# Splitting the last matmul of a decode layer 6 to 8 instead of 4 to 10 over the TensorE column groups, and issuing two of its blocks earlier

## The chip, the cores and the metric

One core of a Trainium2 chip. The metric is device microseconds (us) of one execution; a time is the median of several executions. The profile's span runs from the first to the last instruction and is about 1.8 us shorter than the measured time.

## The reference

A decode step of one transformer layer, for four rows (batch 4, one token): modulated layer norm, attention over the last 1024 cached keys and values, then a feed-forward part with ReLU. Only its end matters here:

```python
h = layernorm(x) * (1 + cb) + sb
x = x + gb * (relu(h @ w1) @ w2)     # w1: 512 x 1792, w2: 1792 x 512, bf16
```

The kernel reads 32 MB of weights and caches for very little arithmetic.

## The kernel before

All large loads go through one queue, in the order of use. w2 comes last, in five transfers. It has 14 **blocks** of 128 rows, numbered m = 0 to 13.

```python
nc.sync.dma_start(out=w1_sb, in_=B_w1.rearrange("(p t) n -> p t n", t=DT))
W2_CHUNKS = [(0, 4), (4, 4), (8, 3), (11, 2), (13, 1)]      # (first block, blocks)
for (m0, e) in W2_CHUNKS:
    nc.sync.dma_start(out=w2_dst[:, m0 * D:(m0 + e) * D],
                      in_=B_w2[m0 * P:(m0 + e) * P, :].rearrange("(q e) n -> q (e n)", e=e))
```

The product with w2 has four useful rows, so the kernel uses TensorE in column groups of 32. A block takes two steps (x = 0, 1), and in each step one matmul in each of two groups. The lower pair of groups (0, 1) accumulates into `z_ps`, the upper pair (2, 3) into `za_ps`.

```python
def closing(parts):
    for x in range(NX):                                   # NX = 2
        for (ps, q, j, src, rhs, start, stop, cols) in parts:
            for g in range(2):
                q0 = (q + g) * CG                         # column group q + g, CG = 32
                nc.tensor.matmul(out=ps[q0:q0 + CG, cols], lhsT=rows(src, j, x), rhs=rhs(2 * x + g),
                                 start=start and x == 0, stop=stop and x == NX - 1, tile_position=(0, q0))
...
for (m0, m1) in [(0, 8), (8, FT)]:                        # FT = 14
    ffn1(m0, m1)                                          # uT32 = relu(h @ w1), in two parts
for m in range(ZA):                                       # ZA = 4
    closing([zpart(m), zpart(ZA + m)])                    # upper m beside lower 4 + m
zc = work.tile([2 * CG, DH2], f32, name="zc")             # the side path
nc.scalar.copy(out=zc[:], in_=za_ps[2 * CG:P, :])
nc.vector.tensor_tensor(out=zc[:], in0=zc[:], in1=gb2[:], op=ALU.mult)
nc.vector.tensor_tensor(out=zc[:], in0=zc[:], in1=x12_ps[:], op=ALU.add)
for m in range(2 * ZA, FT):
    closing([zpart(m)])                                   # blocks 8 to 13, lower
zg = work.tile([2 * CG, DH2], f32, name="zg")
nc.vector.tensor_tensor(out=zg[:], in0=z_ps[:], in1=gb2[:], op=ALU.mult)
nc.vector.tensor_tensor(out=res[:], in0=zg[:], in1=zc[:], op=ALU.add)
# then res is stored from two queues
```

Of the kernel before, what the change touches and what calls it, by code (L numbers as in the profile page):

```python
# [17 lines left out]
def kernel(  # L18
# [23 lines left out]
    FT = Dff // P  # L42
# [13 lines left out]
    DH2 = D // NH  # L56
# [65 lines left out]
    w2_sb = w12[:, DT * Dff:DT * Dff + FT * D].rearrange("p (m n) -> p m n", m=FT)  # L122
# [54 lines left out]
    uT32 = const.tile([P, FT, CP], bf16, name="uT32")  # L177
# [8 lines left out]
    def rows(tile3, j, x):  # L186
        return tile3[:, j, NX - x:NX - x + CG]

    def closing(parts):
        for x in range(NX):  # L190
            for (ps, q, j, src, rhs, start, stop, cols) in parts:
                for g in range(2):
                    q0 = (q + g) * CG
                    nc.tensor.matmul(out=ps[q0:q0 + CG, cols], lhsT=rows(src, j, x), rhs=rhs(2 * x + g),  # L194
                                     start=start and x == 0, stop=stop and x == NX - 1, tile_position=(0, q0))
# [272 lines left out]
        return w1_sb[:, t, m0 * P + m - m0:(m0 + e) * P:e]  # L468


    ZA = 4
    z_ps = psA.tile([2 * CG, DH2], f32, tag="t", name="z_ps")
    za_ps = psA.tile([P, DH2], f32, tag="t", name="za_ps")

    def ffn1(m0, m1):
        u_ps = psA.tile([P, m1 - m0, 2, B], f32, tag="t", name=f"u_ps_{m0}")
        for m in range(m0, m1):
            for t in range(DT):
                nc.tensor.matmul(out=u_ps[:, m - m0].rearrange("p s b -> p (s b)"), lhsT=w1_cols(t, m),
                                 rhs=ab[:, t].rearrange("p s b -> p (s b)"), start=(t == 0), stop=(t == DT - 1))  # L480
        us = work.tile([P, m1 - m0, B], f32, name=f"us_{m0}")
        nc.vector.tensor_tensor(out=us[:], in0=u_ps[:, :, 0, :], in1=rstd2[:].unsqueeze(1).to_broadcast([P, m1 - m0, B]),
                                op=ALU.mult)
        nc.vector.tensor_tensor(out=us[:], in0=us[:], in1=u_ps[:, :, 1, :], op=ALU.add)
        nc.vector.tensor_scalar_max(out=put(uT32[:, m0:m1, :]), in0=us[:], scalar1=0.0)

    def zpart(m):
        upper = m < ZA
        return (za_ps if upper else z_ps, 2 if upper else 0, m, uT32, lambda j: w2_sb[:, m, j * DH2:(j + 1) * DH2],
                m in (0, ZA), m in (ZA - 1, FT - 1), slice(None))  # L490

    for (m0, m1) in [(0, 8), (8, FT)]:
        ffn1(m0, m1)
    for m in range(ZA):
        closing([zpart(m), zpart(ZA + m)])
    zc = work.tile([2 * CG, DH2], f32, name="zc")
    nc.scalar.copy(out=zc[:], in_=za_ps[2 * CG:P, :])
    nc.vector.tensor_tensor(out=zc[:], in0=zc[:], in1=gb2[:], op=ALU.mult)
    nc.vector.tensor_tensor(out=zc[:], in0=zc[:], in1=x12_ps[:], op=ALU.add)
    for m in range(2 * ZA, FT):  # L500
        closing([zpart(m)])

    zg = work.tile([2 * CG, DH2], f32, name="zg")
# [36 lines left out]
```

## Time and profile before

| | before |
|---|---|
| time, median of 3 runs | 85.59 us (85.52 to 85.87) |
| span of the profiled execution | 83.9 us |
| landings of the w2 transfers 1 to 5, from the trace | 77.16, 78.45, 79.36, 80.03, 80.35 us |
| first and last z matmul start | 78.49, 80.58 us |
| zg, res, store issued | 80.93, 81.25, 81.56 us |

A landing can be read off the page's views: the start of the issue in the queue's timeline plus the time from issue to landing.

### The profile page before, as it was taken

Reading aid. Unit: us, or ns where it says so; the run is one execution under the profiler, and the core shown is the slowest. Engines: PE = TensorE matmul, PEld = TensorE weight load, DVE = VectorE, ACT = ScalarE, POOL = GpSimd, SP = SyncE. Lnnn points to the kernel's source line nnn. Section 1 sums busy time; section 2 is a strip of 40 time slices with the busy share of each in tenths; the row PEclk is TensorE's granted clock in tenths of the full one; section 3 lists DMA queues with packets and bytes.
Section 4 is the critical chain, followed back from the end, with each engine's and each line's share of the span. In section 5 each row is a group of like instructions: output and inputs, shape, how many; then the busy total and the mean of one; then the engine's idle time right before and its main releaser. Section 6 shows DMA issues by size and latency. Waiting matters only on the chain.

```text
span 83.9 us, 2373 instructions
## 1 busy us (share of the span) xinstructions
PE 56.3 (67%) x1064; PEld 47.6 (57%) x1064; DVE 26.3 (31%) x76; ACT 23.9 (28%) x38; POOL 5.9 (7%) x21
## 2 busy tenths in 40 slices
PE   0001006999972989999999932999737579577850
PEld 0001006995862973997777702999737249567640
DVE  0201300348033010264566576850001320251350
ACT  3201001654302000497779809530100010001000
POOL 5894000000000000000000000000000000000000
PEclk9999999999995555599999999569655555555555
DMA  2799999998999999999999999999999999999600
GB/s 40 287 474 431 390 430 442 512 500 360 391 387 410 430 422 426 403 426 422 418 414 422 422 418 426 410 426 418 422 410 430 410 430 437 408 384 402 233 4 2
DMA packets 4258, 32.14 MB, mean 383 GB/s; under 512 B 529, under 2 KB 665, under 8 KB 1305
## 3 DMA queue, kind: packets, MB, share of 16 engines
q1 hardware_dynamic: 4192, 31.99, 92.1%
q8 instruction: 8, 0.13, 0.6%
q10 hardware_dynamic: 24, 0.01, 0.0%
q0 software_dynamic: 32, 0.00, 0.0%
q14 instruction: 2, 0.01, 0.0%
HBM read 31.99 MB, written 0.00 MB: 382 GB/s over the span
## 4 chain that ended last, share of the span: by engine, by line
DMA 61%; PE 30%; DVE 3%; issue 1%; SPq 1%; ACT 1%; DVEq 0%
DMA v<-in_A_v_cache_dram 24%; DMA w<-in_B_w_dram 23%; PE ktp L225 14%; DMA k<-in_A_k_cache_dram 14%; PE qT_ps L322 4%; PE sc_ps L237 3%; PE z_ps L194 3%; PE mT L273 2%; PE mT L275 1%; PE m_ps L259 1%; PE m_ps L262 1%; PE st_ps_var L289 1%; PE gb_ps L194 1%; SPq L93 0%; SPq L92 0%
## 5 line engine op out<-in xcount | busy, mean ns | idle before, releaser
L225 PE MATMUL ktp<-ident_k,k 128*128 128x128 bf16 x256 | 18.8, 245 | 5.6 <-DMA k<-in_A_k_cache_dram 5.6
L225 PEld LDWEIGHTS <-k 128*128 128x128 bf16 x256 | 17.8, 112 | 8.2 <-DMA k<-in_A_k_cache_dram 5.7
L230 ACT COPY kT<-ktp 128x1024 bf16<-128x1024 bf16 x16 | 15.6, 1015 | 17.9 <-PE ktp L225 16.8
L228 DVE COPY kT<-ktp 128x1024 bf16<-128x1024 bf16 x16 | 11.1, 692 | 16.8 <-PE ktp L225 16.5
L360 PE MATMUL oT_ps<-pT,v 128*128 128x16 bf16 x256 | 7.1, 172 | 2.0 <-issue 2.0
L360 PEld LDWEIGHTS <-v 128*128 128x128 bf16 x256 | 7.1, 100 | 2.0 <-issue 2.0
L237 PE MATMUL sc_ps<-kT,qpad 128*32 128x512 bf16 x64 | 5.6, 445 | 0.4 <-DVE qpad L326 0.4
L377 PE MATMUL pT_ps<-ident_bf,p_rep 128*128 128x128 bf16 x32 | 3.3, 287 | 2.9 <-DVE p_rep L371 2.9
L200 PE MATMUL tp<-ident_bf,cx_sb 8*128 8x8 bf16 x4 | 0.3, 176 | 7.3 <-POOL xs L180 7.3
L377 PEld LDWEIGHTS <-p_rep 128*128 128x128 bf16 x32 | 2.9, 131 | 3.4 <-DVE p_rep L371 3.4
L322 PE MATMUL qT_ps<-hT,wq_sb 128*128 128x4 bf16 x128 | 3.6, 167 | 1.4 <-DVE ab L315 1.4
L200 PEld LDWEIGHTS <-cx_sb 8*128 8x128 bf16 x4 | 0.2, 116 | 7.3 <-DMA cx_sb<-in_A_x_dram 7.3
L322 PEld LDWEIGHTS <-wq_sb 128*128 128x128 bf16 x128 | 3.5, 104 | 1.5 <-DMA wq_sb<-in_A_wq_dram 1.5
L429 ACT COPY y<-y_ps 128x256 f32<-128x256 f32 x1 | 0.4, 372 | 9.3 <-DVE y L428 9.3
L402 DVE TENSOR_TENSOR oT_sb<-oT_ps,rb 128x128 bf16<-128x128 f32 x1 | 0.3, 291 | 7.8 <-PE oT_ps L360 7.8
L436 PEld LDWEIGHTS <-wo_sb 128*128 128x128 bf16 x64 | 2.5, 120 | 0.4 <-DMA wo_sb<-in_A_wo_dram 0.4
L371 DVE TENSOR_TENSOR p_rep<-e_sb,mi 128x512 int32<-128x512 int32 x4 | 2.5, 687 | 0.7 <-ACT e_sb L366 0.7
L436 PE MATMUL y_ps<-o,wo_sb 128*128 128x4 bf16 x64 | 2.4, 173 | 0.4 <-DMA wo_sb<-in_A_wo_dram 0.4
L432 PEld LDWEIGHTS y_ps<-sel_b,y 128*128 128x128 f32 x8 | 1.8, 328 | 1.4 <-DVE y L428 1.4
L194 PEld LDWEIGHTS <-uT 128*32 128x32 bf16 x56 | 2.2, 136 | 0.8 <-DMA w<-in_B_w_dram 0.4
L194 PE MATMUL z_ps<-w,uT 128*32 128x128 bf16 x40 | 2.4, 307 | 0.2 <-DMA w<-in_B_w_dram 0.2
L424 PE MATMUL y_ps<-wo_sb,o 128*32 128x512 bf16 x16 | 1.9, 628 | 0.9 <-DVE o L415 0.9
(113 smaller groups left out, 54.6 us busy)
## 6 DMA issues: line engine op xcount, KB each, us to landing
k<-in_A_k_cache_dram SPq DMA_DIRECT2D x8, 1024.0 KB, 28.4
v<-in_A_v_cache_dram SPq DMA_DIRECT2D x8, 1024.0 KB, 19.8
wq_sb<-in_A_wq_dram SPq DMA_DIRECT2D x1, 4096.0 KB, 23.6
wo_sb<-in_A_wo_dram SPq DMA_DIRECT2D x4, 1024.0 KB, 20.0
wmod_sb<-in_w_mod_dram SPq DMA_DIRECT2D x1, 2304.0 KB, 9.5
w<-in_B_w_dram SPq DMA_DIRECT2D x1, 1792.0 KB
w<-in_B_w_dram SPq DMA_DIRECT2D x2, 512.0 KB, 20.1
wmod_sb<-in_w_mod_dram SPq DMA_DIRECT2D x1, 768.0 KB, 4.4
```

What stands on the lines that cost most here:

```text
L194: nc.tensor.matmul(out=ps[q0:q0 + CG, cols], lhsT=rows(src, j, x), rhs=rhs(2 * x + g), start=start and x == 0, stop=stop and x == NX - 1, ...
L225: nc.tensor.transpose(out=tp[:, ii, :], in_=k_tiles[gi][:, iq * IQ + ii, :], identity=ident_k)
L228: nc.vector.tensor_copy(out=dst, in_=tp[:])
L230: nc.scalar.copy(out=dst, in_=tp[:])
L237: nc.tensor.matmul(out=sc_ps[hw * CG:(hw + 1) * CG, half * HALF:(half + 1) * HALF], lhsT=qpad[:, b, par, hw, :], rhs=kT[:, half * (NI // 2 ...
L322: nc.tensor.matmul(out=qT_v[:, hq, :], lhsT=wq_sb[:, t, hq * Dh:(hq + 1) * Dh], rhs=hT[:, t, :], start=(t == 0 and hq == 0), stop=(t == DT ...
L360: nc.tensor.matmul(out=oT_ps[:, hw, par].rearrange("p b r -> p (b r)"), lhsT=v_tiles[h][:, i, :], rhs=pT[:, i, c0:c0 + B * rep], start=(fi ...
L371: nc.vector.tensor_tensor(out=p_w[:, ws, :], in0=e_w[:, ws].unsqueeze(2).to_broadcast([P, WQ // 2, B]), in1=mi4[:].unsqueeze(1).to_broadca ...
L377: nc.tensor.transpose(out=tp[:, ii, :], in_=p_rep[:, i // 2, :, i % 2], identity=ident_bf[:])
L424: nc.tensor.matmul(out=y4_ps[q0:q0 + CG, :], lhsT=o4[:, l, g % 2, g // 2, :], rhs=wo_sb[:, g, l, :], start=(g == 0 and l < 4), stop=(g == ...
L432: nc.tensor.matmul(out=y_ps[:, t, :], lhsT=y4[:, t, :], rhs=sel_b[:], start=(t == 0), stop=False)
L436: nc.tensor.matmul(out=y_ps[:, m, :], lhsT=wo_sb[:, g, l, m::DT], rhs=o4[:, l, g % 2, g // 2, 0:B], start=False, stop=(g == NP - 1 and l = ...
```

## The change

Its intent is to even out the two pairs of groups, so that fewer matmuls stand in series in the lower pair, and to use the idle time before the second w2 transfer lands for two blocks of the first.

```diff
-    ZA = 4
+    ZUP = (0, 1, 2, 3, 6, 7)
+    ZLOW = tuple(m for m in range(FT) if m not in ZUP)
...
-    for m in range(ZA):
-        closing([zpart(m), zpart(ZA + m)])
+    for ms in [(0,), (1,), (2, 4), (3, 5), (6,), (7,)]:
+        closing([zpart(m) for m in ms])
...
-    for m in range(2 * ZA, FT):
+    for m in range(8, FT):
         closing([zpart(m)])
```

The rest of the diff lets `zpart` pick the pair of groups and the start and stop flags by these lists.

## The prediction

> **What bounds the kernel now.** I read the page's chain that ended last first, then its 40 slices, then the end of the kernel in the chain in order of time and the timeline, and last the table of DMA issues, to set each landing beside the instruction that needs it. The page first:
>
> ```profile
> PEclk9999999999995555599999999569655555555555
> DMA  2799999998999999999999999999999999999600
> ...
> DMA 61%; PE 30%; DVE 3%; issue 1%; SPq 1%; ACT 1%; DVEq 0%
> ```
>
> The reader is to see that the 16 DMA engines are nine tenths busy from the start up to the 37th slice (a slice is 83.9/40 = 2.1 us, so until about 78 us), that DMA is 61% of the chain, and that TensorE runs at a granted clock of 0.5 in all of the last part. This is a kernel that streams weights and caches and ends with what the last bytes leave to do. The last bytes are w2, in five transfers: blocks 0-3, 4-7, 8-10, 11-12 and 13. The change only touches the matmuls on w2, so the end is what I have to read. The chain in order of time:
>
> ```profile
> 58.98 19.47 DMA w<-in_B_w_dram
> 78.45 0.04 issue
> 78.49 0.29 PE z_ps L194 x2
> ...
> 79.44 1.47 PE z_ps L194 x26
> 80.91 0.02 issue
> 80.93 0.29 DVE zg L504
> 81.22 0.02 issue
> 81.25 0.28 DVE res L506
> ```
>
> The second w2 transfer (issued at 58.98) lands at 78.45 and lets the z matmuls go; after them come two DVE steps and the store. Between 78.49 and 80.91 the chain names only PE. That makes TensorE look like the limit there, and the change would then pay. The timeline shows how it works (start, duration):
>
> ```profile
> 77.96 0.29 PE L194 MATMUL za_ps<-w,uT 128*32 128x128 bf16 x2 [0.17 <-DVE uT L485]
> 78.49 0.29 PE L194 MATMUL z_ps<-w,uT 128*32 128x128 bf16 x2 [0.24 <-DMA w<-in_B_w_dram]
> 78.50 0.30 PE L194 MATMUL za_ps<-w,uT 128*32 128x128 bf16 x2
> 78.58 0.32 PE L194 MATMUL z_ps<-w,uT 128*32 128x128 bf16 x2
> 78.58 0.32 PE L194 MATMUL za_ps<-w,uT 128*32 128x128 bf16 x2
> ...
> 79.12 0.32 PE L194 MATMUL za_ps<-w,uT 128*32 128x128 bf16 x2
> 79.48 0.26 ACT L497 COPY zc<-za_ps 64x128 f32<-64x128 f32 x1 [3.56 <-PE za_ps L194]
> ```
>
> A **round** is one matmul in each column group that is in use: 0.107 us from one start to the next ((79.12 - 78.58)/5), whether two groups work or four. Every block needs two rounds in its pair of groups (x = 0 and 1). Before, the lower pair (z_ps) has ten blocks, 20 rounds, and the upper (za_ps) four. Eight z rounds, blocks 4-7, start from 78.49 to 79.22. Then comes block 8, which lies in the third transfer. The issue table and the queue's timeline, narrowed to that issue, and the timeline around 79.4:
>
> ```profile
> w<-in_B_w_dram SPq DMA_DIRECT2D x1, 384.0 KB, 17.9
> ```
>
> ```profile
> 61.49 0.33 SPq L129 DMA_DIRECT2D w<-in_B_w_dram  x1
> ```
>
> ```profile
> 79.22 0.48 PE L194 MATMUL z_ps<-w,uT 128*32 128x128 bf16 x4
> 79.41 0.13 PEld L194 LDWEIGHTS <-uT 128*32 128x32 bf16 x3
> ```
>
> The third transfer lands at 61.49 + 17.9 = 79.39 (rounded), and the next weight loads start at 79.41, though the round that began at 79.22 has streamed its columns by 79.22 + 0.107 = 79.33. Matmul ends are modelled and overlap, so neither chain nor waits show this **0.08 us wait for block 8**; the landing does. In the same way the fourth transfer (256 KB, issued at 64.11, 15.9 us to landing) lands at 80.01, just where block 11 is due: 79.41 + 6 rounds x 0.107 = 80.05. So TensorE is on the chain there, but it is paced by arrivals: block 8 can't start before 79.4, nor block 11 before 80.0.
>
> **What the Trainium skill says.** "TensorE: Matmul & The Clock Gate", Part 3 "The mechanism": "MATMULs are pc-monotone in start AND end"; only weight loads are pulled ahead. So a matmul that waits for a landing holds up those behind it, of other column groups too. The trace agrees: block 0's x = 1 matmuls, whose data were there by 77.96, start at 78.50, behind block 4's wait. "TensorEngine Tiling (Array Packing)", Key Properties: different tiles can run weight loads and matmuls in parallel. The trace agrees: two z and two za matmuls start within 0.01 us and the round is no longer for it. "DMA: Bandwidth & Descriptors", "Why a DMA increments its semaphore by 16 and not by 1": only the full 16 means that all data landed. The kernel waits once for each transfer, so a block can't start on part of one; the trace has single waits at 78.45 and 79.4, but does not show the counts.
>
> **The change part by part.** By the instruction order of both kernels, PE has the same 2020 rows, the same 56 matmuls on w2 and the same waits; DVE and ACT have the same rows in the same order. Nothing is added or removed. Two things move.
>
> 1. Blocks 0 and 1 go first, alone, with the x = 0 matmul pair of block 2 also ahead of the wait for the second transfer: five rounds in the upper groups, from 77.96, about 0.08 for the first and 0.107 for the others (0.08 from the first step above, 78.50 to 78.58): the fifth starts at 77.96 + 0.08 + 3 x 0.107 = 78.36. Before, one round was issued in that gap. So four rounds (0.43 us of TensorE's time) leave the stretch after 78.49 and use idle time. This works, I expect.
>
> 2. Blocks 6 and 7 move from lower to upper: lower has 8 blocks (16 rounds), upper 6 (12). But they are issued as (6,), (7,), with no lower partner. From 78.49: z4 x0 with za2 x1; z4 x1 with za3 x0; z5 x0 with za3 x1; z5 x1 with za6 x0; then za6 x1, za7 x0, za7 x1 alone. That is 7 rounds before block 8 where there were 8, since the za stream is one round ahead. The seventh starts at 78.49 + 0.08 + 5 x 0.107 = 79.11 and block 8's lower groups have been free since about 79.0. So block 8 could start at 79.11 instead of 79.32: in the lower groups 0.107 us for the saved round and another 0.107 because block 8 may run beside za7.
>
> What these are worth: **nothing on the path**, as block 8 still can't start before 79.39. The wait grows from 0.08 to about 0.3 us and the rest stays: block 8 at 79.41, blocks 8-13 in 12 rounds, the last z matmul ending at 80.9, then zg, res and the store. The transfers are issued from 56 to 67 us, long before, and in the same order, so no landing moves. The za path does not move either: the last za round starts at 79.11, as now (79.12), so the copy starts at 79.48, and the two DVE steps on zc end about 80.4, half a microsecond before zg needs DVE. Sum: 0.00 us, give or take 0.03.
>
> **The rivals.** (a) *TensorE is the bound of the end* and the landing at 79.39 is near enough to give way in some runs. Then the most to be had is the wait after the last z round: were all landed, before would go on at 79.32, the changed kernel at 79.11, so 0.1 us for each of the two terms, 0.2 us or 0.25% at most; 85.4 us. For it: the chain names only PE there. Against it: the landing is later than both of these, and DMA has been the limit for the 78 us before, so it comes no earlier because of this change. (b) *The shift of two blocks to za makes the side path late*: the copy of za_ps then comes later and ends after z_ps. It would need over 0.5 us; I count none. If TensorE gave no overlap to za-only rounds, it would be about 0.1 us, still hidden. (c) *A denser burst of matmuls makes the granted clock drop or delays the DVE steps on uT*, which read PSUM while TensorE now writes za_ps. The clock is already 0.5 from before these matmuls to the end; the second uT write is needed only by block 8 (it ends at 78.46), with 0.9 us to spare. Worth 0 to 0.05 us. (d) A scatter of landings between executions of both kernels, which has nothing to do with the change: the runs of before go from 85.52 to 85.87.
>
> **Range and chances.** The centre is before's median, 85.59, less a small share (a fifth) of rival (a): 85.57. The range is mostly the spread of the runs, which is 0.35 us for one kernel; the gain of (a) lies inside it. 85.3 to 85.9. A change of 2% is 1.7 us; the whole stretch from the second landing to the last z matmul is 2.4 us, and the change can't touch over 0.2 of it. So within 2% is nearly certain.
>
> **What would show it right or wrong.** In the changed profile: five za rounds from about 77.96 to 78.4 ahead of the wait for the second transfer; two z blocks in that stretch instead of four; after them za alone to about 79.1; then a gap on TensorE, longer than before, until the third transfer lands at about 79.4; the same 12 rounds to about 80.9; the copy of za_ps at about 79.5 and off the chain. I am wrong if block 8 starts well before the third landing of the profile before (the landing moved), if the za copy ends after zg could start, or if za-only rounds take over 0.107 us, so that block 8 is late by more than 0.05 us.

## The result, and the profile after

| | before | changed |
|---|---|---|
| median of 6 runs | 85.61 us (85.52 to 86.04) | 85.62 us (85.53 to 85.67) |
| second w2 landing | 78.45 | 78.26 |
| third landing, and start of block 8 | 79.36, 79.41 | 79.19, 79.23 |
| last z matmul ends | 80.89 | 80.69 |
| from the second landing to that end | 2.44 | 2.43 |

The ratio of the changed kernel to before is 0.9989, with a 95% interval of 0.9967 to 1.0012: the same. The profiled execution of the changed kernel is 0.2 us ahead of that of before at the second landing already, ahead of anything that changed; so I compare times from that landing on.

The page of the changed kernel, the granted clock and DMA by slices and the chain by engines:

```profile
PEclk9999999999985555799999998589555555555555
DMA  2899999998999999999999999999999999999600
...
DMA 63%; PE 27%; DVE 4%; issue 1%; SPq 1%; ACT 1%; DVEq 0%
```

DMA is busy to the same slice, and TensorE's clock is 0.5 in the last part again. The timeline of the changed kernel (start, duration, engine, line, operation, count):

```profile
77.79 0.72 PE L194 MATMUL za_ps<-w,uT 128*32 128x128 bf16 x10 [0.15 <-DVE uT L486]
...
78.30 0.29 PE L194 MATMUL z_ps<-w,uT 128*32 128x128 bf16 x2
...
78.60 0.32 PE L194 MATMUL z_ps<-w,uT 128*32 128x128 bf16 x2
78.62 0.64 PE L194 MATMUL za_ps<-w,uT 128*32 128x128 bf16 x8
...
79.23 0.45 PEld L194 LDWEIGHTS <-uT 128*32 128x32 bf16 x9 [0.25 <-issue]
79.29 0.26 ACT L498 COPY zc<-za_ps 64x128 f32<-64x128 f32 x1 [3.58 <-PE za_ps L194]
```

The ten za matmuls (five rounds) fill the gap ahead of the second landing. Four z rounds follow, from 78.30 to 78.60, where before had eight; then there are only za rounds. Now there is an idle mark on the weight loads: 0.25 us ahead of 79.23. The view puts it down to "issue", which means only that it found no releaser. The third transfer's issue, in the table of issues and in the queue's timeline, says what it is:

```profile
w<-in_B_w_dram SPq DMA_DIRECT2D x1, 384.0 KB, 17.7
```

```profile
61.46 0.33 SPq L129 DMA_DIRECT2D w<-in_B_w_dram  x1
```

61.46 + 17.7 = 79.16 (79.19 in the trace), and block 8 starts 0.04 us after that, as it did before. The end of the chain is the old one:

```profile
80.71 0.02 issue
80.73 0.29 DVE zg L505
81.03 0.02 issue
81.05 0.28 DVE res L507
```

### The profile page after: what moved, and what is told of

Read it like the earlier page. It is cut to its first block, busy times and chain, and to the rows that moved or that the text cites. A ratio compares the mean times of both kernels' runs of the same rounds, so it can differ in the third digit from the quotient of the medians.

```text
span 83.7 us, 2373 instructions
## 1 busy us (share of the span) xinstructions
PE 56.1 (67%) x1064; PEld 47.0 (56%) x1064; DVE 26.5 (32%) x76; ACT 23.8 (28%) x38; POOL 6.0 (7%) x21
## 4 chain that ended last, share of the span: by engine, by line
DMA 63%; PE 27%; DVE 4%; issue 1%; SPq 1%; ACT 1%; DVEq 0%
DMA w<-in_B_w_dram 26%; DMA v<-in_A_v_cache_dram 24%; DMA k<-in_A_k_cache_dram 14%; PE ktp L225 9%; PE qT_ps L322 4%; PE sc_ps L237 2%; PE z_ps L194 2%; PE mT L273 2%; PE mT L275 2%; PE u_ps L480 1%; PE za_ps L194 1%; PE m_ps L259 1%; PE m_ps L262 1%; PE st_ps_var L289 1%; PE gb_ps L194 1%
## 5 line engine op out<-in xcount | busy, mean ns | idle before, releaser
L225 PE MATMUL ktp<-ident_k,k 128*128 128x128 bf16 x256 | 18.2, 240 | 5.6 <-DMA k<-in_A_k_cache_dram 5.6
L225 PEld LDWEIGHTS <-k 128*128 128x128 bf16 x256 | 17.2, 110 | 8.2 <-DMA k<-in_A_k_cache_dram 5.7
L237 PEld LDWEIGHTS <-qpad 128*32 128x32 bf16 x64 | 1.3, 103 | 2.2 <-DVE qpad L326 0.7
```

Of the source, the lines that this page charges most:

```text
L225: nc.tensor.transpose(out=tp[:, ii, :], in_=k_tiles[gi][:, iq * IQ + ii, :], identity=ident_k)
L237: nc.tensor.matmul(out=sc_ps[hw * CG:(hw + 1) * CG, half * HALF:(half + 1) * HALF], lhsT=qpad[:, b, par, hw, :], rhs=kT[:, half * (NI // 2 ...
```

## The experiments

**Theory:** block 8 waits for the third landing, in both kernels, and all after it follows. **Rival:** TensorE's own rounds set the end, and the change merely fails to shorten them. A round is the time of one matmul in each group in use, 0.107 us. Kernels are compared only within the same rounds. The times:

| run | median | before, same rounds | ratio (95%) |
|---|---|---|---|
| after_pad1 | 85.54 | 85.59 | 0.9994 (0.9974 to 1.0014) |
| after_pad4 | 85.90 | 85.59 | 1.0024 (1.0004 to 1.0044) |
| before_pad4 | 86.41 | 85.59 | 1.0095 (1.0072 to 1.0118) |
| after_late3 | 86.27 | 85.59 | 1.0075 (1.0058 to 1.0093) |
| ahead_only | 85.43 | 85.56 | 0.9987 (0.9973 to 1.0000) |
| six_only | 85.41 | 85.56 | 0.9985 (0.9971 to 1.0000) |
| before_w2first | 89.39 | 85.56 | 1.0452 (1.0436 to 1.0468) |
| after_w2first | 89.45 | 85.56 | 1.0459 (1.0440 to 1.0478) |
| paired_w2first | 89.43 | 85.50 | 1.0455 (1.0441 to 1.0470) |
| upperfirst_w2first | 89.72 | 85.50 | 1.0494 (1.0479 to 1.0508) |
| after_fine | 85.71 | 85.50 | 1.0020 (1.0007 to 1.0034) |
| before_fine | 85.73 | 85.50 | 1.0024 (1.0012 to 1.0037) |

All gave correct results. By the 2% line, the four kernels with w2first in their name are slower than before and all others the same; where I call a smaller difference real, its interval excludes 1.

### Moving the landing: after_late3

```diff
-    W2_CHUNKS = [(0, 4), (4, 4), (8, 3), (11, 2), (13, 1)]
+    W2_CHUNKS = [(0, 4), (4, 4), (8, 5), (13, 1)]
```

> The changed kernel with blocks 8 to 12 in one transfer (five blocks, 640 KB) instead of two, so block 8 needs what was the fourth landing, 0.64 us later. The matmuls and their order are the same. Theory (a landing holds block 8): block 8 starts 0.64 us later and the whole rest with it, minus 0.04 to 0.1 us for stalls that vanish: 86.1 to 86.2 us. Rival (TensorE's rounds set the end and the landing is near but not binding): less than 0.4 us more, as a spare of TensorE's work would first have to be used up.

Measured: 86.27 us, 0.75% or 0.64 us over before. The third landing came 1.52 us after the second, where the changed kernel has 0.93: 0.59 us later. The last z matmul ended 3.03 us after the second landing instead of 2.43: 0.59 us later before rounding. The timeline now names the wait:

```profile
80.18 0.29 PE L194 MATMUL z_ps<-w,uT 128*32 128x128 bf16 x2 [0.54 <-DMA w<-in_B_w_dram]
```

The end moved with the landing, one to one, though no matmul and no order changed. A rival with slack on the landing is out. The expected 86.1 to 86.2 us was a little low: from the start of block 8 to that end it is 1.46 us in both traces, so the stalls that I took off were worth nothing, and the stretch from the end of res to the end of the span grew from 2.33 to 2.37 us (the last experiment shows why).

### Adding TensorE work ahead of block 8: after_pad1, after_pad4, before_pad4

Useless blocks in the lower groups, ahead of block 8, into rows of `za_ps` that nobody reads (n = 1 or 4; each two rounds):

```diff
+    for k in range(n):
+        closing([(za_ps, 0, k, uT32, lambda j: w2_sb[:, k, j * DH2:(j + 1) * DH2], k == 0, k == n - 1, slice(None))])
     zc = work.tile([2 * CG, DH2], f32, name="zc")
```

> The changed kernel with one useless block (two rounds in the idle lower column groups, into a part of za_ps that nobody reads) placed ahead of block 8. Theory (block 8 waits for the third w2 transfer, TensorE has about 0.25 us to spare there): the first useless round runs beside the last za round, the second ends before the landing, block 8 still starts 0.04 us after the landing, time unchanged, 85.6 us. Rival (TensorE's own rounds set the end): 0.11 to 0.21 us more.

Measured: 85.54 us, unchanged; block 8 started 0.04 us after the third landing. As expected. By time alone the rival's lower figure is not excluded (the interval reaches 0.12 us); the start of block 8 in the trace is what speaks against it.

> The changed kernel with four useless blocks (eight rounds of 0.107 us, 0.86 us of TensorE's time, the first beside the last za round) ahead of block 8. Theory: about 0.25 us of it falls into the wait, and the short stalls for the third and fourth transfers (0.04 and 0.05 us) go as well; block 8 starts about 0.56 us later against the second landing than now and the last round about 0.6 us later: about 86.2 us. Rival (TensorE sets the end already): all 0.86 us appear, 86.45 us.

Measured: 85.90 us, only 0.31 us over before's median. From the second landing to the end of the last z matmul it took 2.79 us against 2.43 without the addition, so of 0.86 us added only 0.36 appeared; 0.50 us was hidden. I had expected 0.25.

> The kernel before with the same four useless blocks ahead of block 8. Theory: here TensorE has only 0.08 us to spare, so about 0.8 us appear: 86.4 us, and the changed kernel with the same addition is 0.2 us faster than this one, which is what the change saves on TensorE when no landing hides it. Rival (the change saves TensorE nothing): both equal.

Measured: 86.41 us, 0.82 us more; in the trace 3.21 us against 2.44, so 0.09 us hidden. As expected for before. But the two padded kernels differ by 0.51 us in the medians (0.6 by the ratios), and by 3.21 - 2.79 = 0.42 us in the traces, which is four rounds; not by 0.2. **The change saves TensorE about twice what I had worked out**, and the next lines show why. The timeline of after_pad4:

```profile
78.72 0.32 PE L194 MATMUL z_ps<-w,uT 128*32 128x128 bf16 x2
78.74 1.16 PE L194 MATMUL za_ps<-w,uT 128*32 128x128 bf16 x24
79.68 1.49 PE L194 MATMUL z_ps<-w,uT 128*32 128x128 bf16 x24
```

The 24 za matmuls are four upper rounds (8 matmuls) and the eight useless lower rounds (16; they bear za's name too). In series this would be eleven or twelve rounds, some 1.2 us, before block 8. But block 8 starts at 79.68, nine rounds after the z round at 78.72: that round and the eight useless ones follow each other without a gap. The lower groups did not wait for the three upper rounds (blocks 6 and 7) that stand ahead of the useless ones in program order.

### One part at a time: ahead_only, six_only

```diff
-    ZUP = (0, 1, 2, 3, 6, 7)
+    ZUP = (0, 1, 2, 3)
```

> One part of the change: blocks 0 and 1 first and the order of the change, but blocks 6 and 7 stay in the lower groups (four blocks upper, ten lower). Theory: eight z rounds between the second landing and block 8, as before the change, so block 8 could start about 0.85 us after the second landing and waits for the third, 0.93 us after the second; time unchanged, 85.6 us; za_ps is done earlier by about 0.3 us, which nobody needs.

Measured: 85.43 us against 85.56. Block 8 at 79.22, the third landing at 79.18: same mechanism, same time.

```diff
-    for ms in [(0,), (1,), (2, 4), (3, 5), (6,), (7,)]:
+    for ms in [(0, 4), (1, 5), (2,), (3,), (6,), (7,)]:
```

> The other part: six blocks in the upper groups, but no blocks issued ahead (pairs 0 and 4, 1 and 5, then 2, 3, 6, 7 alone). Theory: after the second landing the upper groups have eleven rounds before block 8, so block 8 starts about 1.07 us after the second landing instead of 0.93, and the last round about 0.1 to 0.15 us later: 85.7 us; the copy of za_ps comes 0.4 us later and ends just before zg can start. Rival (balance between the groups is what counts, whatever the order): no slower than before, 85.6 us or less.

Measured: 85.41 us against 85.56, so not slower, and the expected 0.1 us did not come. Its trace says why. In program order all za matmuls stand ahead of block 8. The timeline:

```profile
78.69 0.64 PE L194 MATMUL za_ps<-w,uT 128*32 128x128 bf16 x8
79.11 0.29 PE L194 MATMUL z_ps<-w,uT 128*32 128x128 bf16 x2
79.11 0.32 PE L194 MATMUL za_ps<-w,uT 128*32 128x128 bf16 x2
79.17 0.34 PE L194 MATMUL z_ps<-w,uT 128*32 128x128 bf16 x2
79.22 0.32 PE L194 MATMUL za_ps<-w,uT 128*32 128x128 bf16 x2
```

The first two z matmuls here are block 8; they start at 79.107, 0.04 us after the third landing, ahead of the last two rounds of za (79.115 and 79.222), which precede them in the program. A matmul of one column group can start ahead of earlier matmuls of another. Neither of these two kernels is shown to be faster than before; both intervals touch 1.

### Taking the landings away: before_w2first, after_w2first

w2 queued ahead of w1, so that every block is there in time and no landing of w2 can hold TensorE (a slower kernel on purpose):

```diff
-    nc.sync.dma_start(out=w1_sb, in_=B_w1.rearrange("(p t) n -> p t n", t=DT))
     for (m0, e) in W2_CHUNKS:
         nc.sync.dma_start(out=w2_dst[...], in_=B_w2[...])
+    nc.sync.dma_start(out=w1_sb, in_=B_w1.rearrange("(p t) n -> p t n", t=DT))
```

> The kernel before with all w2 transfers queued ahead of w1, so that w1 lands last and every block of w2 has long landed when the z matmuls start. Both theories: about 4 us slower, near 89.6 us, since the whole of the first FFN product then follows the last landing. Theory: z rounds run without a stall, 20 rounds from the first to the last.

Measured: 89.39 us, 20 z rounds without a stall from 82.29 to 84.29, as expected.

> The changed kernel with w2 queued ahead of w1. Theory (the blocks issued ahead are free only because TensorE waits for the second transfer): without that wait the change has 23 rounds in series where before has 20, so this is about 0.3 us slower than the kernel before with the same order of transfers, near 89.9 us. Rival (the change makes the z matmuls shorter as such): about 0.2 us faster than it.

Measured: 89.45 us; the two are equal within their intervals. Both the theory (0.3 us slower, by strict order) and the rival (0.2 faster) missed. The timeline:

```profile
82.24 0.40 PE L194 MATMUL za_ps<-w,uT 128*32 128x128 bf16 x4 [0.17 <-DVE uT L486]
82.34 0.30 PE L194 MATMUL z_ps<-w,uT 128*32 128x128 bf16 x2
...
82.66 0.30 PE L194 MATMUL z_ps<-w,uT 128*32 128x128 bf16 x2
82.75 0.64 PE L194 MATMUL za_ps<-w,uT 128*32 128x128 bf16 x8
83.08 0.40 PE L194 MATMUL z_ps<-w,uT 128*32 128x128 bf16 x4
```

Block 4, behind five za rounds in the program, starts with the second (82.34): it overtakes three rounds, six matmuls. Its groups are free again at 82.66 + 0.107 = 82.77. The second part of uT, which block 8 needs, is written by 82.74; in paired_w2first below, block 8 starts 0.06 us after that write, so here it could start at about 82.79. Yet it starts only at 83.08. At that time three za rounds are still ahead of it in the program (83.18, 83.29, 83.39 in the same timeline): again six matmuls. So four lower rounds less (0.43 us) are paid back by a start 0.09 us later and this stop of 0.32 us (of which about 0.02 us is for uT). This gave me a new theory: **a lower matmul may overtake at most six upper ones.**

### Testing the limit: upperfirst_w2first, paired_w2first

```diff
-    for ms in [(0,), (1,), (2, 4), (3, 5), (6,), (7,)]:
+    for ms in [(0,), (1,), (2,), (3,), (6,), (7,), (4,), (5,)]:
```

> w2 queued ahead of w1, all six upper blocks (twelve rounds) issued ahead of the first lower block. Three theories on the order of matmuls of different column groups. Strict program order: the first lower round starts with or after the twelfth upper one, 1.15 to 1.26 us after the first; end about 0.75 us later than in before_w2first, 90.1 us. No order between groups: first lower round at once, 16 rounds, about 0.4 us faster, 89.0 us. New theory from the last runs (a lower matmul may overtake at most six upper ones, three rounds): the first lower round starts with the ninth upper one, 0.83 us after the first, and the end is about 0.43 us later than in before_w2first: 89.8 us.

Measured: 89.72 us, in a different call from before_w2first: 0.33 us above it by the medians, 0.36 by the ratios to before. The timeline:

```profile
82.72 0.75 PE L194 MATMUL za_ps<-w,uT 128*32 128x128 bf16 x10
83.16 0.40 PE L194 MATMUL z_ps<-w,uT 128*32 128x128 bf16 x4
83.25 0.32 PE L194 MATMUL za_ps<-w,uT 128*32 128x128 bf16 x2
```

The first z matmul starts at 83.16, 0.84 us after the first za at 82.32, beside the ninth upper round, with three upper rounds still to come. The place is the expected one; strict order (1.15 us or more) and no order at all are both out. The weight loads show the same limit with w2 in its usual place: in six_only the first load for block 8 (known by its wait for the second part of uT) starts at 78.91, with three upper rounds (79.01, 79.12, 79.22) still to come, though its groups were free from 78.46 + 0.107 = 78.57. One thing is not separated: each block that was held is the first of a transfer and itself waits for a semaphore, though one that had been met by then. What a lower block that waits for nothing does behind more than six upper matmuls, no run shows. The whole came out 0.07 us quicker than expected.

```diff
-    for ms in [(0,), (1,), (2, 4), (3, 5), (6,), (7,)]:
+    for ms in [(0, 4), (1, 5), (2, 8), (3, 9), (6, 10), (7, 11), (12,), (13,)]:
...
-    for m in range(8, FT):
-        closing([zpart(m)])
```

> w2 queued ahead of w1 as in before_w2first, six blocks upper and eight lower, all pairs issued together (0 and 4, 1 and 5, 2 and 8, 3 and 9, 6 and 10, 7 and 11, then 12, 13), so nothing waits and nothing is far behind in the queue. New theory (a column group takes one round in 0.107 us, and what counts is the number of lower rounds once no landing holds them): 16 lower rounds instead of 20, at most one short stall for the second part of uT, so 0.3 to 0.43 us faster than before_w2first: near 89.0 us. Rival (moving blocks to the upper groups is worth nothing on TensorE): 89.4 us.

Measured: 89.43 us, the same as before_w2first, a miss in time. TensorE did what was expected: from the first z start to the last z end 2.01 us instead of 2.32, 0.31 us less. But the side path took its place:

```profile
83.84 0.26 ACT L498 COPY zc<-za_ps 64x128 f32<-64x128 f32 x1 [8.12 <-PE za_ps L194]
84.14 0.28 DVE L499 TENSOR_TENSOR zc<-zc,gb 64x128 f32<-64x128 f32 x1 [1.34 <-ACT zc L498]
84.45 0.28 DVE L500 TENSOR_TENSOR zc<-zc,x_ps 64x128 f32<-64x128 f32 x1
84.66 0.27 DVE L503 TENSOR_TENSOR zg<-z_ps,gb 64x128 f32<-64x128 f32 x1
```

z_ps is finished at 84.32, but zg starts at 84.66 with no idle mark: DVE takes it behind the second zc step, which starts at 84.45. za_ps ends 0.47 us later here (83.79) than in before_w2first (83.32), and copy and two steps then take 0.9 us. So the shorter z path was not on the path that sets the end any more.

### Bringing the third landing closer: after_fine, before_fine

```diff
-    W2_CHUNKS = [(0, 4), (4, 4), (8, 3), (11, 2), (13, 1)]
+    W2_CHUNKS = [(0, 4), (4, 4), (8, 2), (10, 2), (12, 1), (13, 1)]
```

> The changed kernel with the w2 transfers after the second cut into blocks 8-9, 10-11, 12 and 13, so that block 8 needs 256 KB instead of 384 KB. Theory: the third landing comes about 0.3 us sooner and block 8 with it (about 0.6 us after the second landing), but block 13 lands when it did, and its two rounds follow that landing: last round start about 0.1 us earlier than in the changed kernel: 85.5 us, a gain too small to tell from the spread by time alone. Rival (the third landing alone sets the end): 0.3 us faster.

> The kernel before with the same finer transfers. Theory: block 8 starts when its eight z rounds are through, about 0.85 us after the second landing (TensorE holds it now, not the landing), so it is 0.25 us later than in after_fine, but the landing of block 13 is the same and takes most of that back: last round about 0.05 us before that of the kernel before, 0.05 to 0.08 us after that of after_fine; 85.55 us.

Measured: 85.71 and 85.73 us against 85.50 for before in these rounds, both slower, by 0.20% and 0.24%. In the stretch that I had reasoned about, it went as expected. In after_fine block 8 started 0.67 us after the second landing (0.97 in the changed kernel) and the last z matmul ended 2.36 us after it, where the changed kernel took 2.43: 0.07 us gained. In before_fine block 8 came 0.87 us after it, held by its eight z rounds, and the end at 2.37. The gain is small because the last transfer then holds its block: in after_fine it lands at 80.20 and block 13 starts at 80.24. But the stretch from the end of res to the end of the span grew from 2.33 to 2.55 us (2.54 in before_fine). SyncE's waits in this last stretch, changed kernel and then after_fine:

```profile
SPq L536 <- DMA out_dram<-res: 0.6, 1, 0.6
```

```profile
SPq L536 <- DMA out_dram<-res: 1.0, 1, 1.0
```

At the end SyncE waits for all DMA semaphores in a fixed list, six instructions of two semaphores each. In the changed kernel the stores' semaphores are in the last two, and the others have been passed by the time the stores land. The sixth w2 transfer shifts the queue's ring of semaphores by one, SyncE's store gets one from the second instruction of the list, and four more follow it at about 0.06 us each. So 0.07 us was gained and 0.22 lost, +0.15 us, where 0.1 to 0.2 was measured. The 0.22 us itself is measured. That the list is its cause, the traces bear out at three places in it: from the landing of SyncE's store to the end of the list it is 0.08 us in the changed kernel, where no instruction follows that store's own; 0.14 us in after_late3, which has one transfer less and one instruction after it; and 0.31 us in after_fine, with four after it. No run moved the semaphore alone. The same cutting with the number of transfers kept (say, by merging two earlier loads) was not run and could gain at most about 0.07 us.

## Why the prediction was right

- **The landing bounds the end.** Right. Block 8 starts 0.04 us after the third landing in both kernels, and after_late3 moves that landing and the end together by 0.59 us. It is not the only landing that counts: in after_fine it came 0.30 us sooner and the end only 0.07 us, since block 13 then waited for the last transfer. Of my signs of being wrong, "block 8 starts well before the third landing of the profile before" came true by the clock of the span (79.23 against 79.36), but the second landing was 0.19 us earlier too: from there the third came after 0.93 us, where before had 0.91.
- **Blocks 0 and 1 fill the idle gap.** Right: five za rounds from 77.79, ahead of the landing at 78.26.
- **The side path stays hidden.** Right: za's copy starts 1.03 us after the second landing in both, and zg does not wait for zc. paired_w2first shows that this rival is real elsewhere.
- **Rounds before block 8.** This term was mis-sized. I had "7 rounds before block 8 where there were 8", so that TensorE would be ready "at 79.11 instead of 79.32". That assumed strict program order between column groups. What counts is the lower rounds alone, as long as no more than six upper matmuls are overtaken: four instead of eight, which frees 0.43 us where I had 0.21. The time could not show this error, because the landing hides either figure: for this term the hit says nothing. In the changed kernel the lower groups are free at 78.60 + 0.107 = 78.71 and wait 0.52 us for 79.23; the padded kernels show the same, 0.50 us hidden against 0.09.
- **Rival (a).** I called 0.2 us the most that could be had without the landing. after_pad4 against before_pad4 shows 0.42 us in the traces and 0.51 in the medians. With all of w2 landed early it is about nothing (after_w2first: 0.02 us less from the first za to the last z end than before_w2first), because the lower groups then stand behind the upper rounds issued ahead. Neither mattered here, since the landing hides all of it.
- **The Trainium skill on order** ("TensorE: Matmul & The Clock Gate", Part 3 "The mechanism"). I took one example as agreement: block 0's second step behind block 4's wait. That is a matmul behind one whose semaphore had not come, and such a wait does hold up what follows. It does not show that matmuls behind a *busy column group* are held, and the runs show that up to six of them need not be.
- **The clock.** No effect: the mean granted clock is 0.772 and 0.768 in the two profiled executions, 0.5 in the last part of both.
- **Slips that change nothing.** In the DMA row that I quoted the first two slices are 2 and 7 tenths, so DMA is not nine tenths busy from the very start. The four matmuls that "start within 0.01 us" of each other do so in the round at 78.49; at 78.58 they spread over 0.02 us. Block 11 has a small wait of its own: its groups are free at about 80.03 and it starts at 80.07, 0.04 us after its landing. The 2020 rows of PE are not the count of a trace: the page has 1064 matmuls and 1064 weight loads for both kernels.

## What to carry to other kernels

Set the landing of each late transfer beside the first instruction that needs it before counting what an engine saves: an engine that the chain names may be paced by arrivals, and overlapping modelled matmul ends hide the gap. To measure slack that no view shows, add a known amount of useless work and see how much of it appears. And count matmuls for each column group by itself, mind how far one group can run ahead of another, and look at the fixed end of the program when you change the number of DMAs.

## What the Trainium skill lacked or had wrong

- "TensorE: Matmul & The Clock Gate", Part 3 "The mechanism", says that matmuls start and end in program order. Starts here do not across column groups: in six_only block 8 starts at 79.107, ahead of two earlier-issued rounds at 79.115 and 79.222; the time of after_pad4 (0.31 us for 0.86 us of added lower rounds) fits this and not strict order. Ends are modelled in these traces, so nothing is said of them.
- The same section has no limit for it. after_w2first and upperfirst_w2first show lower matmuls held until only six upper ones (three rounds of two) were still ahead of them, and six_only shows a weight load held at the same place; what the limit counts, and whether it holds for a block that waits for no semaphore, was not separated.
- No page that I read has the cost of one more DMA at the end of a program: 0.22 us more from the last DVE step to the end (2.33 to 2.55 us) when the store's semaphore moved forward in the closing list of waits, at about 0.06 us for each of the four instructions after it.
